# Output products two slots later, and the copy of the transposed maxima between two exponentials, in a kernel of two Fourier and two attention layers

## The chip, the cores and the metric

The kernel runs on one core of one Trainium2 chip. The metric is the device time of one execution in microseconds (us), the median of several. A profile of one execution stands beside it: a page of tables and a trace of every instruction. In its rows PE is the tensor engine (PEld are its weight loads), DVE the vector engine, ACT the scalar engine, POOL the GpSimd engine, and SP the queue from which the kernel issues nearly all of its transfers. [...]

## The reference

Four layers on a matrix of 2048 rows (tokens) and 640 columns: a Fourier layer (A), an attention layer (B), and both once more. Each adds its result to its input; in front of each stands a layer norm.

```python
def _A_ref(x, dft_seq_re, dft_seq_im, dft_hid_re, dft_hid_im):
    a = jnp.einsum("bsd,ed->bse", x, dft_hid_re)
    b = jnp.einsum("bsd,ed->bse", x, dft_hid_im)
    return jnp.einsum("ts,bse->bte", dft_seq_re, a) - jnp.einsum("ts,bse->bte", dft_seq_im, b)

def _B_ref(x, wqkv, wo):            # S = 2048, D = 640
    H = 32; Dh = D // H; W = 256    # 32 heads of 20 columns, a window of 256 rows
    q, k, v = ...                   # x @ wqkv, split by heads
    scores = jnp.einsum("bhqd,bhkd->bhqk", q, k) * (Dh ** -0.5)
    mask = (idx[:, None] - idx[None, :] >= 0) & (idx[:, None] - idx[None, :] < W)
    p = _softmax(jnp.where(mask, scores, -1e9))
    return jnp.einsum("bhqk,bhkd->bhqd", p, v)... @ wo

x = x + _A_ref(_layernorm(x), ...);  x = x + _B_ref(_layernorm(x), ...)
x = x + _A_ref(_layernorm(x), ...);  x = x + _B_ref(_layernorm(x), ...)
```

## The kernel before, in words

The Fourier layers are `spectral`, the attention layers `attention(0)` and `attention(1)`. Every product is made from fp16 halves (high and low part), three matmuls for one. All that the change touches lies in `attention`, which runs twice: from about 566 to 1070 us of the profiled span as layer 0, and from about 1580 us to the end as layer 1.

**Slots.** `attention` writes out its order by hand. Its main loop runs over `G`, and `now[0] = g = 2 * G` is the slot number; every pass takes two slots. The 2048 rows are cut into eight blocks of 256 rows (`b = g // 32`), and a pass works on four heads of 128 rows. A group of heads goes through a pipeline of passes:

- `scores(G)` and `largest(G)`: products of queries and keys, and their largest value for each row (DVE). After every second pass `part_tops` packs the maxima in fp16 halves (POOL, tile `tops`).
- `hand_on(n)`, HAND_LAG = 3 passes after the first of its two: PE turns the packed maxima (`hp`), ACT copies them to `ht` (L1176), SP stores `ht` to DRAM (`htd`). Two slots later `take_tops(n)` loads them as two extra rows of the query stack `qs` (`qs<-htd` in the trace), for which SP waits until the store has landed.
- `by_key(G)`, KEY_LAG = 8 passes behind: the scores once more, keys on the partitions, with the maxima subtracted by the two extra rows; then `probabilities(G, 1)` and `probabilities(G, 0)`, the two exponentials (ACT, L1211), behind which POOL masks the corners.
- `values(n)`, VALUE_LAG = 11: the products with v, the copy `pvs` (ACT), and `back(n)`, the turn back: PE turns the result to rows on partitions (`pf<-idf,pvs` in the trace), DVE divides by the sums (`r`, `o`), and POOL writes it in fp16 halves to `os` (a cast, L1262, and a subtraction, L1263). A block has eight groups `n`, so `back(8 * b + 7)` completes the block. `values(n)` stands in slot 4n + 22, and `back(n)` at the end of the same slot where a filler unit ran in it, else in the next pass.

**Filler units.** Beside this pipeline each pass runs one filler unit of 15 matmuls (`run_unit`; in some passes two, in some none). Kinds: `qk` (queries and keys of a block to come, 15 matmuls of 256 columns, `pf<-early,big`), `v` (`pf<-big,early`), `out` (the output product of 128 rows, two units, `pf<-bo,ot`, ended by DVE's `x` at L935), in layer 0 also `next` (first products of the next Fourier layer), and `last` (output products of the last block in three pieces of columns, 0-3, 3-4 and 4-5, made from PE transposes of `os`). A unit can be taken when its slot `at` has come and what it needs (`need`) is done; even passes prefer the wide kinds (all but `qk`), and of those the one with the smallest due slot goes first. In layer 1 the odd passes from slot 224 to 255 run no unit.

**Output of a block.** When `back` completes a block b below 7, it queues for each half m of the block (128 rows, number i = 2b + m)

```python
at, due, kind = now[0] + OUT_STEPS[0] + OUT_STEPS[2] * m, 2 * NP * (b + 2) + OUT_STEPS[1], ("out", b)
need = [(i - 2, 2)] if i > 1 else []
outs.append((at, need, partial(out_turn, i)))
fill.append(Unit(at, out_tile(i), kind, due + 3 * m + 2, [(i, 1)] + ["wo"] * (layer == 0)))
```

`out_turn(i)` is run by the loop in the first pass from slot `at` on in which the buffers allow it: SP issues a transposing DMA of `os` into `ot` (DMA_TRANSPOSE `ot<-os`) and the load `x<-x2d`. The unit `out_tile(i)` can be taken from six slots after `out_turn` (TURN_LAG). Within a pass SP gets first the store of `hand_on`, then the loads of `take_tops`, then the held loads of the stacks `qs` and `ks` (`qs<-qkd`, `ks<-qkd`), then `out_turn`. For the last block `back` queues the pieces as `last` units with a first slot of `now[0] + LAST_STEPS[0]`, at least 258 for the first half's early pieces and 272 for the second half.

**Orders.** PE's instructions and SP's loads are chained, so both keep the order in which the program writes them. On ACT, DVE and POOL a planner with costs of its own places instructions, unless a mark binds them: `in_line("act")` puts an instruction behind the last one that was marked on ACT. The exponentials are marked so, the copy L1176 is not.

Of the kernel before, what the change touches and what calls it, by code (L numbers as in the profile page):

```python
# [14 lines left out]
AF = mybir.ActivationFunctionType  # L15
# [21 lines left out]
FILL_LAST = 8  # L37
QK_SLOT = 20
NEXT_STEPS = (10, 22)
OUT_STEPS = (4, 40, 8)  # L40
LAST_STEPS = (1, 258)
LAST_FROM = 3
HAND_LAG = 3
KEY_LAG = 8
# [28 lines left out]
def body(ctx: ExitStack, tc: tile.TileContext, x_in, cmat, whid, wqkv, wo, out):  # L73
    nc = tc.nc
# [107 lines left out]
    def load(out, in_):  # L182
        with ExitStack() as order:
            if in_turn[0] and loads:
                order.enter_context(tc.issue_after(loads[-1]))
            elif floor:
                order.enter_context(tc.issue_after(floor[-1]))
            i = nc.sync.dma_start(out, in_)
        loads.append(i.ins)
# [17 lines left out]
    def new_f():  # L207
        return pf_.tile([P, 512], F32, tag="f", name="pf", bufs=2)
# [615 lines left out]
    def attention(layer, proj, dst, final):  # L824
        with ExitStack() as st:
# [294 lines left out]
            TOP, PT, topped, marks = {}, {}, [None], {}  # L1120

            @contextmanager
            def in_line(name):
                with ExitStack() as order:
                    if name in marks:
                        order.enter_context(tc.issue_after(marks[name]))
                    yield

            def place(g):

                b, r = divmod(g, 2 * NP)
                return 2 * b + r // 2 % 2, 2 * (r // 4) + r % 2
# [37 lines left out]
            def hand_on(n):  # L1170

                b, q = divmod(n, NP // 2)
                hp = new_f().bitcast(F16)[:16, :P]
                transpose(hp, tops[n % 2], idh)
                ht = sb.tile([16, P], F16, tag="ht", name="ht", bufs=3)
                nc.scalar.activation(ht, hp, AF.Copy)  # L1176
                load(ht_d[n % 4], ht)
                handed.append((now[0] + 2, partial(take_tops, n)))

# [21 lines left out]
            def probabilities(G, pi):  # L1201
                i, p0 = place(2 * G)
                first = max(0, 2 - i)
                n, k = divmod(G, 2)
                if k == 0 and pi:
                    PT[n] = sb.tile([P, 4, 6, P], F32, tag="ptq", name="ptq", bufs=2)
                q = PT[n]
                a0 = 3 * (i % 2)
                o = q[:, :, a0 + first:a0 + 3].rearrange("p (e l) a c -> p l e a c", e=2)
                with in_line("act"):  # L1210
                    marks["act"] = nc.scalar.activation(o[:, pi], tps[pi][:, :, first:], AF.Sigmoid, bias=shift, scale=alpha[:, 0:1]).ins  # L1211
                if pi:
                    return
                if i >= 2:
                    nc.gpsimd.affine_select(out=q[:, :, a0], in_=q[:, :, a0], pattern=[[0, 4], [-1, P]], base=0,  # L1215
                                            channel_multiplier=1, compare_op=OP.is_gt, fill=0.0)
                ins = nc.gpsimd.affine_select(out=q[:, :, a0 + 2], in_=q[:, :, a0 + 2], pattern=[[0, 4], [1, P]],  # L1217
                                              base=0, channel_multiplier=-1, compare_op=OP.is_ge, fill=0.0).ins
                if G == NG // 2 - 1 and not final:
                    hidden.after = ins  # L1220
# [24 lines left out]
            def back(n):  # L1245
# [20 lines left out]
                if last and d1 > k * 4 * DH // P and (d1 > 2 or k > LAST_FROM):  # L1266
                    for m in range(2):
                        step0 = max(now[0] + LAST_STEPS[0], NG + 2 * KEY_LAG if m else LAST_STEPS[1] if d1 < ND else 0)
                        fill.append(Unit(step0, last_out(2 * b + m, lastd[0], d1), "last", NS + 2 * d1 + m, [(2 * b + m - 2, 2)]))
                    lastd[0] = d1  # L1270
                elif k == NP // 2 - 1 and not last:
                    for m in range(2):
                        i = 2 * b + m
                        at, due, kind = now[0] + OUT_STEPS[0] + OUT_STEPS[2] * m, 2 * NP * (b + 2) + OUT_STEPS[1], ("out", b)
                        need = [(i - 2, 2)] if i > 1 else []
# [8 lines left out]
            def queue_qk(b):  # L1284
                for w in (1, 0):
                    for ct in range(ND):
                        need = [("rows", b, t) for t in range(2)] if b > 1 else []
                        fill.append(Unit(0, proj_qk(b, w, ct), ("qk", b), 2 * NP * (b - 1) + QK_SLOT, need, ns=15 * 109))
# [28 lines left out]
            for G in range(NS // 2 + 1):  # L1317
                now[0] = g = 2 * G
                b, r = divmod(g, 2 * NP)
                if g == NG:  # L1320
                    floor.append(loads[-1])
                if g < NG:
                    if r == 0:
                        flush(("qk", b))
                        if b == 0:
                            queue_qk(1)
                            queue_v(1)
                keyed = 0 <= G - KEY_LAG < NG // 2
                if g < NG:
                    scores(G, (0,))  # L1330
                if keyed:
                    by_key(G - KEY_LAG)
                if g < NG:
                    scores(G, (2, 1))
                if g < NG:
                    largest(G, 0)
                if keyed:
                    probabilities(G - KEY_LAG, 1)
                if g < NG:
                    largest(G, 1)  # L1340
                    if G % 2:
                        part_tops(G // 2)
                if keyed:
                    probabilities(G - KEY_LAG, 0)
                n = due(G, HAND_LAG)
                if n is not None:
                    hand_on(n)
                if turned_back:
                    with in_line("dve"):
                        back(turned_back.pop())  # L1350
                c = 2 if g == 0 else b + 3
                if g < NG and c < NBQ and (g == 0 or r == X2_STEP):
                    wanted.append(c)
                if wanted and x2s and g >= x2s[0] + 4 * (g > 0):
                    slow.append(rows_norm(wanted.pop(0), x2s.pop()))
                    x2s.clear()
                if slow:
                    normed_at[0] = g
                if wanted and not slow and not x2s and g >= normed_at[0] + FREE_STEPS:
                    x2s += [g, [keep.tile([P, D], F32, tag="res0", name="x2", bufs=2) for t in range(2)]]  # L1360
                    for t in range(2):
                        load(x2s[1][t], x2_d[2 * wanted[0] + t])
                if g < NG and r == ROWS_STEP:
                    flush(("v", b))
                    if b < NBQ - 2:
                        proj.new_rows(b + 2)
                        queue_qk(b + 2)
                        queue_v(b + 2)
                if g < NG and r == HIDDEN_STEP:
                    if b == NBQ - 1 and not final:  # L1370
                        flush(("v", b))
                        hidden = Hidden(xu_d)
                        pieces = hidden.pieces()
                        for k in range(2):
                            fill.append(Unit(g + NEXT_STEPS[k], hidden.stage(k, None), "next", NG + k))
                for _ in range(STEPS[layer][G % 2]):
                    slow_step()
                run_later()
                for _ in range(PIECES):
                    next(pieces, None)  # L1380
                while handed and handed[0][0] <= now[0]:
                    handed.popleft()[1]()
                run_held(1 << 20)
                if outs and outs[0][0] <= g and all(done.get(k, 1 << 20) + FREE_STEPS <= g for k in outs[0][1]):
                    outs.pop(0)[2]()
                n = due(G, VALUE_LAG)
                if n is not None:
                    for part in range(2):
                        values(n, part)
                    turned_back.append(n)  # L1390
                ran = False
                if not (G % 2 and NG - 2 * NP <= g < THIN_TO[layer]):
                    ran = run_unit(G % 2 == 0)
                if G % 2 and g < NG and left() and 2 * left() > must_to() - r:
                    ran = run_unit() or ran
                if ran and turned_back:
                    with in_line("dve"):
                        back(turned_back.pop())
# [40 lines left out]
```

## Time and profile before

| what | value |
|---|---|
| median of 3 runs (lowest to highest) | 2080.46 us (2077.89 to 2085.85) |
| the profiled execution: its time, its span | 2077.48 us, 2075.8 us |
| PE busy | 1991.0 us, 96% of the span |
| DVE, POOL, ACT busy | 1567.5, 1469.5, 1116.1 us |
| mean share of the 16 DMA engines, bytes moved | 50.5% in the main queue, 311.10 MB |
| mean granted clock of PE | 0.996 |

A row of the timeline has the start, the length, the engine, the line, the operation, out<-in by the program's names, the shapes, how many instructions were merged into the row, and in brackets the idle time of the engine before the row with what ended it. A row of SP tells how long the queue was with an issue, not how long the transfer took. In a row of a table by stretches stand, after the stretch and its length, the busy time of each engine with the number of instructions, then the granted clock of PE (1.00 is full speed), the share of the DMA engines and GB/s. All matmuls and transposes have line L126, a helper's, so they are told apart by their tiles.

### The profile page before, as it was taken

The page shows a single profiled execution, that of the slowest core. Times are in us where ns is not written, and L with a number is a line of the kernel's source. Part 1 is how long each engine was busy: PE and PEld are TensorE (multiplying, and loading weights), DVE is VectorE, ACT ScalarE, POOL GpSimd, SP SyncE. Part 2 cuts the span into 40 slices and gives each one's busy share as a digit, 9 for nine tenths or more (in the row PEclk, how much of TensorE's full clock was granted, in tenths as well). Part 3 has the DMA queues.
Part 4 walks back from the last instruction along what each step waited for, and adds up shares of the span by engine and source line. Part 5 has one row for each costly group of instructions (what it writes and reads, how often), then busy time and mean ns, then how long its engine had stood idle before and what let it go on. Part 6 is the DMA issues. An engine that isn't in the chain of part 4 may idle for free.

```text
span 2075.8 us, 55781 instructions
## 1 busy us (share of the span) xinstructions
PE 1991.0 (96%) x21881; PEld 1450.0 (70%) x21881; DVE 1567.5 (76%) x3261; ACT 1116.1 (54%) x1971; POOL 1469.5 (71%) x2162
## 2 busy tenths in 40 slices
PE   6999999999999999999989999999999989999997
PEld 4777777776766777777657777777677667777765
DVE  8888878768688898767538779777867878876682
ACT  5444555534257667766644444444342657666674
POOL 5777788868467777865547778777784767776653
PEclk9999999999999999999999999999999999999999
DMA  7556467565545354445435555454845455544232
GB/s 271 182 200 205 161 216 237 169 250 196 143 105 126 99 131 114 99 97 127 134 124 177 168 169 190 152 162 145 304 144 132 93 107 112 129 105 103 78 79 62
DMA packets 280508, 311.10 MB, mean 150 GB/s; under 512 B 107572, under 2 KB 214836, under 8 KB 271156
## 3 DMA queue, kind: packets, MB, share of 16 engines
q1 hardware_dynamic: 279668, 306.88, 50.5%
q8 instruction: 171, 2.80, 0.6%
q14 instruction: 93, 0.76, 0.1%
q10 hardware_dynamic: 576, 0.66, 0.1%
HBM read 201.72 MB, written 83.46 MB: 137 GB/s over the span
## 4 chain that ended last, share of the span: by engine, by line
PE 73%; DVE 13%; ACT 4%; issue 4%; DMA 3%; POOL 2%; SPq 0%; DVEq 0%; ACTq 0%; POOLq 0%
PE pf L126 32%; PE y L126 13%; PE x L126 12%; PE z L126 8%; PE sk L126 5%; PE sq L126 3%; DVE cc L536 3%; ACT ptq L1211 2%; DVE sq L1156 2%; DVE m L1158 2%; DMA res<-accd 1%; DVE res L559 1%; DVE lnt L151 1%; DVE lnst L139 1%; DVE x L935 1%
## 5 line engine op out<-in xcount | busy, mean ns | idle before, releaser
L126 PEld LDWEIGHTS <-cc 128*128 128x128 f16 x5376 | 524.4, 98 | 214.5 <-issue 14.8
L1211 ACT ACTIVATE ptq<-sk,shift,alpha 128x768 f32<-128x768 f32 (+2 forms) x512 | 471.9, 946 | 149.5 <-PE sk L126 76.0
L126 PEld LDWEIGHTS <-big 128*128 128x128 f16 x4320 | 412.4, 98 | 128.6 <-issue 24.3
L1158 DVE TENSOR_REDUCE m<-sq 128x2 f32<-128x512 f32 (+1 forms) x512 | 345.6, 675 | 19.1
L533 ACT ACTIVATE cc<-cs 128x512 f16<-128x512 f32 x256 | 153.7, 624 | 262.0 <-POOL cs L526 149.4
L126 PE MATMUL pf<-early,big 128*128 128x256 f16 x2400 | 289.2, 274 | 0.8 <-ACT qf L365 0.5
L1215 POOL TENSOR_SCALAR_AFFINE_SELECT ptq<-ptq 128x512 f32<-128x512 f32 x224 | 142.8, 637 | 186.8 <-ACT ptq L1211 185.6
L126 PE MATMUL y<-zc,cc 128*128 128x320 f16 x1728 | 262.8, 299 | 3.2 <-DVE pf L559 3.2
L536 DVE SCALAR_TENSOR_TENSOR cc<-cs,cc 128x512 f16<-128x512 f32 x256 | 249.5, 983 | 7.9 <-ACT cc L533 7.8
L1156 DVE COPY_PREDICATED sq<-mask,sk 128x256 f32<-128x256 int32 x448 | 189.4, 423 | 58.1 <-PE sq L126 56.8
L536 DVE SCALAR_TENSOR_TENSOR cc<-cq,cc 128x512 f16<-128x512 f32 x192 | 206.9, 1079 | 0.1
L126 PE MATMUL pf<-ptq,v 128*32 128x128 f32 (+1 forms) x3840 | 185.9, 332 | 8.1 <-DVE x L935 5.5
L126 PE MATMUL z<-zc,cc 128*128 128x320 f16 x1152 | 177.7, 299 | 6.6 <-DVE res L559 5.6
L126 PE MATMUL x<-zc,cc 128*128 128x320 f16 x1152 | 177.7, 299 | 0.0
L1217 POOL TENSOR_SCALAR_AFFINE_SELECT ptq<-ptq 128x512 f32<-128x512 f32 x256 | 166.3, 649 | 14.0 <-ACT ptq L1211 13.9
L126 PEld LDWEIGHTS pf<-ptq,v 128*32 128x32 f32 x3840 | 111.6, 111 | 53.2 <-DVE x L935 7.4
L365 ACT ACTIVATE qf<-pf 128x256 f32<-128x256 f32 x160 | 61.2, 383 | 157.2 <-PE pf L126 121.1
L126 PE MATMUL pf<-big,early 128*128 128x320 f16 x960 | 141.4, 300 | 1.0 <-ACT ht L1176 1.0
L525 POOL TENSOR_TENSOR cs<-cq 128x512 f32<-128x512 f32 x64 | 87.2, 1363 | 69.3 <-DVE cc L536 68.6
L126 PE MATMUL pf<-bo,ot 128*128 128x320 f16 x840 | 126.5, 304 | 8.4 <-DMA ot<-os 5.2
L126 PEld LDWEIGHTS <-qs 62*128 62x128 f16 x2688 | 90.8, 94 | 60.2 <-issue 55.7
L126 PEld LDWEIGHTS <-ot 128*128 128x128 f16 x960 | 90.4, 99 | 54.7 <-issue 6.8
(141 smaller groups left out, 3517.1 us busy)
## 6 DMA issues: line engine op xcount, KB each, us to landing
cq<-in_cmat_dram SPq DMA_DIRECT2D x64, 1024.0 KB
accd<-res SPq DMA_DIRECT2D x96, 320.0 KB
res<-accd SPq DMA_DIRECT2D x96, 320.0 KB
x<-x2d SPq DMA_DIRECT2D x64, 320.0 KB
qkd<-early SPq DMA_DIRECT2D x160, 128.0 KB
ks<-qkd SPq DMA_DIRECT2D x108, 160.0 KB
qs<-qkd SPq DMA_DIRECT2D x84, 160.0 KB
x2d<-res SPq DMA_DIRECT2D x32, 320.0 KB
```

Source lines behind the costliest of these rows:

```text
L126: i = getattr(nc.tensor, what)(*args, **kw)
L139: nc.vector.bn_stats(st[:, h], x[:, h * 320:(h + 1) * 320])
L151: ts(u, g, g, h, op0=OP.mult, op1=OP.mult)
L365: nc.scalar.activation(f, pf[:, :QB], AF.Copy, scale=down)
L525: g.tensor_tensor(s1, a21, a22, op=OP.add)
L533: nc.scalar.activation(cc[m][:, 0], f, AF.Copy, scale=C_UP)
L536: nc.vector.scalar_tensor_tensor(cc[m][:, 1], f, C_UP, cc[m][:, 0], op0=OP.mult, op1=OP.subtract)
L1156: marks["dve"] = nc.vector.copy_predicated(near[pi][:, :, 0], mask[:, None, :].to_broadcast([P, 2, P]), far).ins
L1158: marks["dve"] = nc.vector.tensor_reduce(TOP[n][:, pi, :, k], near[pi][:, :, :1 + (i >= 1)], axis=AX.XY, op=OP.max).ins
L1211: marks["act"] = nc.scalar.activation(o[:, pi], tps[pi][:, :, first:], AF.Sigmoid, bias=shift, scale=alpha[:, 0:1]).ins
L1215: nc.gpsimd.affine_select(out=q[:, :, a0], in_=q[:, :, a0], pattern=[[0, 4], [-1, P]], base=0, channel_multiplier=1, compare_op=OP.is_gt, ...
L1217: ins = nc.gpsimd.affine_select(out=q[:, :, a0 + 2], in_=q[:, :, a0 + 2], pattern=[[0, 4], [1, P]], base=0, channel_multiplier=-1, compare ...
```

## The change

Two constants and one place. The first slot of `out_turn` and of `out_tile` after a block's last turn back goes from 4 to 6 slots, and that of the pieces of the last block from 1 to 3. `hand_on` is called between the two exponentials instead of behind them, and its copy is bound in ACT's order: behind the first exponential by `in_line("act")`, and, since it sets the mark itself, ahead of the second.

```diff
-OUT_STEPS = (4, 40, 8)
-LAST_STEPS = (1, 258)
+OUT_STEPS = (6, 40, 8)
+LAST_STEPS = (3, 258)
...
@@ hand_on(n)
                 transpose(hp, tops[n % 2], idh)
                 ht = sb.tile([16, P], F16, tag="ht", name="ht", bufs=3)
-                nc.scalar.activation(ht, hp, AF.Copy)
+                with in_line("act"):
+                    marks["act"] = nc.scalar.activation(ht, hp, AF.Copy).ins
                 load(ht_d[n % 4], ht)
...
@@ the loop over G
-                if keyed:
-                    probabilities(G - KEY_LAG, 0)
                 n = due(G, HAND_LAG)
                 if n is not None:
                     hand_on(n)
+                if keyed:
+                    probabilities(G - KEY_LAG, 0)
```

## Prediction, made before the changed kernel ran

> **What bounds the kernel now.** First the page's busy times, then the table by stretches, then PE's own waits and, around them, the timeline.
>
> ```profile
> PE 1991.0 (96%) x21881; PEld 1450.0 (70%) x21881; DVE 1567.5 (76%) x3261; ACT 1116.1 (54%) x1971; POOL 1469.5 (71%) x2162
> ...
> 1000.00:1075.00 75.00, 63.29 (x726) 41.80 (x725) 28.67 (x68) 38.20 (x67) 34.76 (x63) 0.95 0.39 106
> ...
> 1600.00:1700.00 100.00, 89.36 (x1247) 64.67 (x1248) 81.83 (x195) 60.55 (x111) 67.02 (x141) 0.98 0.53 109
> ```
>
> PE works 96% of the span, and its work is not changed. Only its idle time can shrink, and the speed of its matmuls where the clock was halved. Most of the idle time that lies in attention stands in two stretches: 75.00 - 63.29 = 11.7 us where layer 0 ends, and 10.6 us early in layer 1, and the clock drops in both. PE's waits in the two attention layers have one long stop in each, on a transfer and on POOL (rows in parts 1 and 2). So the question is what the new slots do to these two, and what else they move.
>
> **Part 1: the first output unit of layer 1.** Block 0 is complete in slot 50; before, `out_turn(0)` stands in slot 54 and the unit out0 can be taken in slot 60, an even pass, which prefers it. The turn lands too late:
>
> ```profile
> 1671.63 0.37 SPq L188 DMA_DIRECT2D htd<-ht  x1
> ...
> 1672.82 0.38 PE L126 MATMUL pf<-idf,pvs 128*128 128x128 f32 x2
> ...
> 1672.93 3.23 SPq L196 DMA_TRANSPOSE ot<-os  x1
> ...
> 1676.20 0.58 SPq L188 DMA_DIRECT2D x<-x2d  x1
> ...
> 1677.51 1.09 SPq L188 DMA_DIRECT2D qs<-qkd  x2
> 1678.70 0.32 SPq L188 DMA_DIRECT2D htd<-ht  x1
> 1679.21 3.74 PE L126 MATMUL pf<-bo,ot 128*128 128x320 f16 x15 [5.23 <-DMA ot<-os]
> ...
> 1683.23 0.55 SPq L188 DMA_DIRECT2D qs<-htd  x2
> ...
> 1694.91 0.38 PE L126 MATMUL pf<-idf,pvs 128*128 128x128 f32 x2
> ...
> 1679.20:1682.90 3.70, 3.69 (x17) 2.01 (x19) 0.00 (x0) 0.00 (x0) 0.00 (x0) 0.57 0.52 106
> ```
>
> PE stands 5.23 us, and the unit then runs at 0.57 of the clock. After the change the turn stands in slot 56 and out0 is ready in slot 62. In slot 60 no wide unit is ready, so a qk unit of block 3 goes there; out0 takes slots 64 and 68, out1 slots 72 and 84 (before: 60 and 64, 68 and 84). The units of slots 60 to 72 are the same seven in another order. Layer 0 is a twin: out0 waits there for `wo`, and its slots 60 and 62 hold qk units, slot 64 a wide one:
>
> ```profile
> 654.40 0.38 PE L126 MATMUL pf<-idf,pvs 128*128 128x128 f32 x2
> ...
> 654.90 2.83 SPq L196 DMA_TRANSPOSE ot<-os  x1
> ...
> 658.12 0.31 PE L126 MATMUL sk<-ks,qs 62*128 62x128 f16 x4 [0.82 <-ACT ptq L1211]
> ...
> 659.06 1.03 SPq L188 DMA_DIRECT2D qs<-qkd  x2
> ...
> 660.65 1.81 PE L126 MATMUL pf<-early,big 128*128 128x256 f16 x15
> ...
> 664.39 0.27 PE L126 MATMUL sk<-ks,qs 62*128 62x128 f16 x3 [1.55 <-DVE o L1260]
> ...
> 665.15 2.21 PE L126 MATMUL pf<-big,early 128*128 128x320 f16 x15
> ...
> 671.17 0.38 PE L126 MATMUL pf<-idf,pvs 128*128 128x128 f32 x2
> ```
>
> From the turn back of group 9 to that of group 11 layer 0 takes 671.17 - 654.40 = 16.77 us, layer 1 takes 1694.91 - 1672.82 = 22.09 us. The difference is 5.32; of it 2.21 - 1.81 = 0.40 comes back in slot 72, which gets a wide unit for a qk one. That leaves 4.92.
>
> Two corrections. The 1.55 us in layer 0 are the first scores of block 2 (slot 64). The row names DVE, but the last rows of block 2's query stack were issued at 659.06, behind the turn (2.83) and its load, so I read it as that load. After the change these loads stand ahead of the turn, in both layers. I take 1.3 of the 1.55 as gained against the twin in each layer; the bounds are 0 (it is DVE) and 1.55. Against that, the turn now stands behind `qs<-htd` of slot 56, which waits for the store issued at 1671.63. The next store took 1683.23 - 1678.70 = 4.5 us to the load behind it, so SP is free at about 1676.1; 0.55 and 1.09 for two pairs of loads, and the turn is issued near 1677.8. It lands between 3.23 us (its issue alone) and 6.28 us (issue to PE's start, before) later: 1681.0 to 1684.1. PE comes to slot 64's unit at 1672.82 + (665.15 - 664.39) + (664.39 - 654.40) - 1.55 = 1682.0. So it may wait 0 to 2.1 us; I take 1.0. Layer 1: 4.92 + 1.3 - 1.0 = 5.2 us gained, bounds -0.3 (the full stop comes back in slot 64) to 7.3 (with the 1.55 and the 0.82 of the twin gone too). Layer 0: 1.3, bounds 0 to 1.55. The x load and both halves' turns move with `out_turn`; their first users are passes away, as out1 now starts in slot 72. Turns 2 and 3 of layer 1 and turn 12 of both layers move one pass as well, 13 in layer 1; no unit moves nearer to its turn than six slots, and I cost them at nothing, covered by those six slots.
>
> **Part 2: the end of layer 0.** `back(62)` stands in slot 270, and the piece last0:3-4 that needs its `os` could be taken at slot 271, so slot 272 begins with it:
>
> ```profile
> 1040.04 0.34 PE L126 MATMUL pf<-idh,os 128*128 128x128 f16 x3
> ...
> 1041.30 1.52 PE L126 MATMUL sq<-bo,ot 128*128 128x320 f16 x9
> ...
> 1045.99 1.51 PE L126 MATMUL pf<-ptq,v 128*32 128x256 f32 x32
> ...
> 1047.43 2.35 PE L126 MATMUL pf<-bo,ot 128*128 128x320 f16 x16
> ...
> 1049.24 1.26 POOL L525 TENSOR_TENSOR cs<-cq 128x512 f32<-128x512 f32 x1
> ...
> 1049.62 0.38 PE L126 MATMUL pf<-idf,pvs 128*128 128x128 f32 x2
> ...
> 1054.23 0.32 POOL L1262 CAST os<-o 128x160 f16<-128x160 f32 x1
> ...
> 1054.60 0.29 PE L126 MATMUL pf<-idh,os 128*128 128x128 f16 x1 [4.60 <-POOL os L1262]
> ...
> 1065.64 0.28 PE L126 MATMUL pf<-idh,os 128*128 128x128 f16 x2
> ...
> 1067.06 0.27 PE L126 MATMUL pf<-idh,os 128*128 128x128 f16 x2
> ...
> 1054.60:1061.50 6.90, 6.53 (x48) 3.33 (x49) 0.23 (x1) 0.28 (x1) 0.49 (x1) 0.53 0.01 2
> ```
>
> POOL has four sums of the next Fourier layer ahead of the cast, from 1049.24 to 1054.2, and PE stands 4.60 us, then works at 0.53 of the clock. After the change the piece is ready at 273, so slot 272 finishes out13 and goes on with last1:0-3, whose `os` columns are long there. Up to `back(63)` PE then has: 8 matmuls of out13 (half of 2.35, 1.2), six transposes with the wait for their copies (1041.30 - 1040.04 = 1.26), values 1.51, 16 matmuls 2.35: 6.3 us after 1050.0, that is 1056.3, past the cast. Then `back(63)` 0.38, two matmuls 0.3, the piece 1067.06 - 1065.64 = 1.42: last1:3-4 begins 8.4 us after 1050.0, where it now begins at 1065.64, 15.6 us after. Gain 7.2; I take 7.0 for a small wait on a PSUM bank. Bounds: 0 (the four sums then stand before a cast that is still needed at once) to 7.5. What follows, the next Fourier layer, hangs on PE's end here and moves with it.
>
> **Part 3: the end of layer 1.** Turn 13 moves from slot 256 to 258, so out13 runs in slots 264 and 266 instead of 262 and 266/268, and last0:0-3 in 268 and 270 instead of 264 and 266. Slot 262 is now without a unit beside slot 260, and slot 270 gets one. From 272 on nothing changes.
>
> ```profile
> 2040.48 0.61 PE L126 MATMUL sk<-qs,ks 62*128 62x128 f16 x12 [2.05 <-ACT ptq L1211]
> ...
> 2057.50 0.51 PE L126 MATMUL sk<-qs,ks 62*128 62x128 f16 x12 [0.86 <-ACT ptq L1211]
> ...
> 2060.25 0.44 PE L126 MATMUL pf<-idf,pvs 128*128 128x128 f32 x2 [0.80 <-ACT pvs L1243]
> ```
>
> The 0.86 and 0.80 of slot 270 get cover, 1.66 at most; the empty slot 262 costs between 0 (slot 262 has values) and a second 2.05. I take a gain of 0.8, the middle of 0 and 1.66.
>
> **Part 4: the copy.** In ACT's timeline 111 of the 128 copies stand between the two exponentials already, six come before any exponential (n = 0 to 2), and 11 stand behind both (n = 3 to 6 of each layer, 61 and 63 of layer 0, 63 of layer 1). One of the first kind, one of the last, and who waited for the copies in all:
>
> ```profile
> 696.79 0.25 ACT L1176 ACTIVATE ht<-pf 16x128 f16<-16x128 f16 x1
> 696.95 0.97 ACT L1211 ACTIVATE ptq<-sk,shift,alpha 128x768 f32<-128x768 f32 x1
> ...
> 2035.27 0.25 ACT L1176 ACTIVATE ht<-pf 16x128 f16<-16x128 f16 x1
> 2035.57 2.20 PE L126 MATMUL pf<-bo,ot 128*128 128x320 f16 x15 [0.40 <-ACT ht L1176]
> ...
>   PE pf L126: 2.0, 5
> ```
>
> Eleven copies come one exponential earlier and free PE's bank: at most 2.0 us gained. Eleven exponentials start 0.25 later: at most 2.8 lost. I take 0.5 gained.
>
> **Sum.** 5.2 + 1.3 + 7.0 + 0.8 + 0.5 = 14.8 us. The profiled execution took 2077.48 us, 2.98 below the median of 2080.46; that gives 2062.7 by the one and 2065.7 by the other. As the result is a median, I predict 2065. Bounds of the parts: all best, 7.3 + 1.55 + 7.5 + 1.7 + 2.0 = 20.0, gives 2057.5 from the profiled execution.
>
> **A rule about the clock.** In the rows above the clock stands at 0.57 and 0.53 behind stops of 5.23 and 4.60 us. The Trainium skill, page "TensorE: Matmul & The Clock Gate", section "Part 1: The HAM clock gate (the "warmup" mystery)", says that the clock halves after an idle window of about 3.4 us, and that the windows run freely, so that what a stop costs varies between runs. The trace agrees for these two stops. By that rule a median execution might not lose what this one lost to the half clock, 3.74 - 2.21 = 1.5 us in part 1 and up to 6.53 x (1 - 0.53) = 3.1 us in part 2; the sum would be 14.8 - 4.6 = 10.2. I keep 14.8, as the rows show both stops paid for.
>
> **The rivals.**
> - The turn lands late again and the stop moves to slot 64. For it: SP is late there, the store of slot 54 left at 1671.63, about when PE ended slot 58 (1672.82). Against it: PE wants the turn 8 slots after it instead of 6. Part 1 gives -0.3 in layer 1, the sum 9.3: 2071.
> - PE stops at the end of layer 0 all the same, because the planner puts the four sums before another cast. For it: POOL's order is the planner's. Against it: `back(62)` keeps its place, and there are 6.3 us of other work for PE. Sum 7.8: 2073.
> - The change does nothing that counts: both of these, 14.8 - 5.5 - 7.0 = 2.3: 2078.
> - Slower: SP's queue is blocked. The moved turns now stand behind the wait for a landed store and hold up the maxima of the next groups by 3.23 + 0.58 = 3.8 us each; if six of them (0 and 1 of layer 0, 0 to 3 of layer 1) make the products by key wait, 22.9 us are lost and only 8.3 of parts 2 to 4 are gained: 2095. It decides once the loads `qs<-htd` come more than their slack late: ten slots lie between `hand_on` and `by_key`, some 20 us (16.77 us for four passes above). Against it: SP is two passes late there today, and no long stop of PE is for these loads.
>
> **How the numbers follow.** Chances: forecast 0.58, the turn 0.13, the cast 0.13, nothing 0.08, slower 0.08. A measurement of this kernel tells some 0.5%, 10.4 us, from no change: the forecast lies beyond it, the first two rivals within, as does "nothing". With a little for a rival that lands beyond 10.4 us and a little for losses that I have not priced: faster 0.60, same 0.31, slower 0.09. The range goes from 2057, all parts at their best, to 2080, no change, which leaves out the slower case, half of "nothing" and a small tail below. The forecast alone: 2058 to 2070.
>
> **What would show it.** In PE's waits no `DMA ot<-os` of over 2.1 us, and out0 in the pass after the turn back of group 10; PE 94 us busy or more of 1600 to 1700; no 4.6 us stop on `os` near 1050, with last1:0-3 ahead of last0:3-4; a clock of 1.00 in both places; about 128 - 6 copies between exponentials. If the long stops are gone and the time is not down by 10 us, new stops of an order that I took as fixed, on POOL or ACT, make the prediction wrong.

## The result, and the profile after

| kernel | median (lowest to highest), us | the kernel before on the same chip | ratio, 95% interval |
|---|---|---|---|
| changed | 2057.98 (2057.23 to 2061.26) | 2078.24 | 0.9901, 0.9887 to 0.9914 |
| changed, measured again later | 2062.53 (2060.11 to 2066.07) | 2079.89 | 0.9921, 0.9906 to 0.9937 |

The change makes the kernel faster by 20.3 us in the first measurement and by 17.4 us in the second, each against the kernel before on the same chip; the forecast, 2065, was 15.5 below the median it started from (2080.46, of three executions). The profiled execution of the changed kernel took 2060.18 us, its span 2058.5: 17.3 below the span before.

The first row below is the page's busy times after; then come a table by stretches (the end of layer 0, and the 100 us that begin with the work that stood at 1600 before) and two rows of PE's waits in the attention layers and between them: in all, times, longest.

```profile
PE 1986.1 (96%) x21881; PEld 1448.5 (70%) x21881; DVE 1564.7 (76%) x3261; ACT 1114.6 (54%) x1971; POOL 1466.2 (71%) x2162
...
1000.00:1066.00 66.00, 59.45 (x722) 40.33 (x720) 28.08 (x68) 37.57 (x67) 34.35 (x63) 1.00 0.43 120
1591.00:1691.00 100.00, 94.38 (x1311) 68.93 (x1309) 84.75 (x201) 64.66 (x117) 71.94 (x152) 0.98 0.52 111
...
PE sk L126 <- ACT ptq L1212: 9.2, 19, 2.0
...
PE sq L126 <- ACT ot L1027: 2.5, 4, 1.6
```

PE's idle time is 2058.5 - 1986.1 = 72.4 us, before 2075.8 - 1991.0 = 84.8: 12.4 less. The same matmuls were busy for 4.9 us less. Together that is the 17.3. So nearly three quarters come from idle time and the rest from matmuls that no longer run at half clock. (PE's busy times are modelled.) At the end of layer 0 PE is idle for 66.00 - 59.45 = 6.6 us instead of 11.7, in the second stretch for 5.6 instead of 10.6. The two waits shown have the two longest single stops left in attention, 2.0 and 1.6 us; neither `os` nor `ot<-os` stops PE for long.

Where the time went is read from the turns back (`pf<-idf,pvs`). These are the first turn back of layer 1 and the last one of the kernel, before and then after:

```profile
1614.84 0.38 PE L126 MATMUL pf<-idf,pvs 128*128 128x128 f32 x2
2067.08 0.38 PE L126 MATMUL pf<-idf,pvs 128*128 128x128 f32 x2
```

```profile
1605.54 0.38 PE L126 MATMUL pf<-idf,pvs 128*128 128x128 f32 x2
2049.78 0.38 PE L126 MATMUL pf<-idf,pvs 128*128 128x128 f32 x2
```

The changed kernel is 9.3 us ahead where layer 1 begins and 17.3 at the end. The two timelines below show the places. First slots 54 to 68 of both layers, layer 0 and then layer 1:

```profile
655.24 0.38 PE L126 MATMUL pf<-idf,pvs 128*128 128x128 f32 x2
...
659.24 0.72 SPq L188 DMA_DIRECT2D qs<-qkd  x2
...
660.06 2.00 SPq L196 DMA_TRANSPOSE ot<-os  x1
...
663.45 0.48 PE L126 MATMUL sk<-ks,qs 62*128 62x128 f16 x4
...
670.58 0.38 PE L126 MATMUL pf<-idf,pvs 128*128 128x128 f32 x2
...
1664.92 0.38 PE L126 MATMUL pf<-idf,pvs 128*128 128x128 f32 x2
...
1668.59 0.98 SPq L188 DMA_DIRECT2D qs<-qkd  x2
...
1669.67 1.95 SPq L196 DMA_TRANSPOSE ot<-os  x1
...
1674.18 2.21 PE L126 MATMUL pf<-bo,ot 128*128 128x320 f16 x15
...
1681.15 0.38 PE L126 MATMUL pf<-idf,pvs 128*128 128x128 f32 x2
```

The last query-stack loads now leave ahead of the turn, the scores at 663.45 have no stop in brackets, and layer 0 takes 670.58 - 655.24 = 15.34 us where it took 16.77: 1.4 gained. In layer 1 out0 starts without a stop at 1674.18 and runs at full speed (2.21 instead of 3.74); 16.23 us where it took 22.09: 5.9 gained. In slots the turn stood six ahead of out0 and now stands eight. In time it left 1.1 us before PE came for it in the kernel before (1672.93, and 1679.21 - 5.23 = 1673.98), and now leaves 4.5 us before.

Then the end of layer 0:

```profile
1048.34 1.27 POOL L525 TENSOR_TENSOR cs<-cq 128x512 f32<-128x512 f32 x1
1048.72 0.38 PE L126 MATMUL pf<-idf,pvs 128*128 128x128 f32 x2
1048.94 1.25 PE L126 MATMUL pf<-bo,ot 128*128 128x320 f16 x8
...
1050.02 0.33 PE L126 MATMUL pf<-idh,os 128*128 128x128 f16 x3
...
1052.66 2.21 PE L126 MATMUL sk<-bo,ot 128*128 128x320 f16 x15
1053.36 0.32 POOL L1263 CAST os<-o 128x160 f16<-128x160 f32 x1
...
1056.87 0.28 PE L126 MATMUL pf<-idh,os 128*128 128x128 f16 x2
```

POOL still makes the four sums first and casts as late as before, 4.64 us after `back(62)` (before 1054.23 - 1049.62 = 4.61). But PE works through it on out13 and last1:0-3. last1:3-4 begins 1056.87 - 1048.72 = 8.2 us after `back(62)`, before 1065.64 - 1049.62 = 16.0: 7.9 gained.

The end of layer 1 gains another 3.5 us (part 3 below). The four places make 18.7, and 1.4 of it went elsewhere. The changed kernel's profile is 0.8 us behind at group 9 of layer 0. It loses 1.6 between the second and the third turn back of layer 1: 6.85 us there (1611.49 to 1618.34), before 5.23 (1620.79 to 1626.02). A window of half clock stands there that the profile of before hasn't:

```profile
1611.45:1614.87 3.42, 2.21 (x38) 1.00 1.00 259
1614.87:1618.28 3.41, 3.41 (x27) 0.50 0.07 22
```

Some 1.1 us came back in small steps.

### The profile page after: what moved, and what is told of

Same layout as the page of the kernel before. It is cut to its first block, busy times and chain, and to the rows that moved or that the text cites. A ratio compares the mean times of both kernels' runs of the same rounds, so it can differ in the third digit from the quotient of the medians.

```text
span 2058.5 us, 55778 instructions
## 1 busy us (share of the span) xinstructions
PE 1986.1 (96%) x21881; PEld 1448.5 (70%) x21881; DVE 1564.7 (76%) x3261; ACT 1114.6 (54%) x1971; POOL 1466.2 (71%) x2162
## 4 chain that ended last, share of the span: by engine, by line
PE 68%; DVE 15%; issue 5%; DMA 4%; ACT 4%; POOL 4%; SPq 1%; DVEq 0%; ACTq 0%; POOLq 0%
PE pf L126 32%; PE y L126 11%; PE x L126 10%; PE z L126 7%; PE sk L126 5%; DVE cc L536 4%; PE sq L126 3%; ACT ptq L1212 2%; DVE sq L1156 2%; DVE m L1158 2%; DMA res<-accd 2%; DVE res L559 1%; DVE lnt L151 1%; POOL cs L526 1%; DVE lnst L139 1%
## 5 line engine op out<-in xcount | busy, mean ns | idle before, releaser
L126 PE MATMUL x<-big 128*128 128x320 f16 x825 | 122.3, 299 | 2.0 <-DVE big L425 2.0
```

The lines of the kernel that those rows point to most:

```text
L126: i = getattr(nc.tensor, what)(*args, **kw)
```

## The experiments

The slots taken apart: each constant alone, the copy alone, and both constants without the copy.

```diff
-OUT_STEPS = (4, 40, 8)
+OUT_STEPS = (6, 40, 8)
```

> Only OUT_STEPS goes from 4 to 6; LAST_STEPS and the copy stay as before. Theory (three separate gains that add up): 1.4 us less in layer 0 before slot 64's scores, 5.9 less in layer 1 between the turns back of groups 9 and 11, and 0 to 3.4 less at the end of layer 1, where turn 13 moves one pass; in all 7 to 11 us, a median of 2067 to 2071 against 2078.2 before. The stop of 4.6 us on os at the end of layer 0 is still there. Rival (the constants work only together, because what is not used in one place is lost in the next): 2075 to 2078, with the stop on ot gone and another one in its place.

Measured: 2067.09 (2065.26 to 2068.09) against 2077.64, ratio 0.9946 (0.9934 to 0.9959), 10.5 us less. The one long stop left in attention is the other one:

```profile
PE pf L126 <- POOL os L1262: 4.6, 1, 4.6
```

```diff
-LAST_STEPS = (1, 258)
+LAST_STEPS = (3, 258)
```

> Only LAST_STEPS goes from 1 to 3; OUT_STEPS and the copy stay as before. Theory: the gain is at the end of layer 0 alone, 7.2 to 8.5 us, so a median of 2069 to 2071; the stop on ot in layer 1 (5.2 us) stays, and the end of layer 1 moves by -2 to +2. Rival (the cast behind the four sums only gives way because the other two edits shift POOL's order too): a stop on os of 3 us or more is still there and the median lies at 2075 to 2078.

Measured: 2070.35 (2066.91 to 2073.63) against 2077.64, ratio 0.9967 (0.9955 to 0.9979), 7.3 us less, with the mirror image in the waits:

```profile
PE pf L126 <- DMA ot<-os: 4.2, 1, 4.2
```

The two are separate and add up, as the theories of both runs had it: 0.9946 x 0.9967 = 0.9913, between the 0.9901 and the 0.9921 of the whole change. The rival of a gain that only both constants together make falls.

The copy alone (`hand_on` between the exponentials, bound by `in_line`), both constants as before:

> Only the copy's place between the exponentials; both constants as before. Theory: worth next to nothing, 0.5 us less with -2.0 and +2.8 as bounds: 2076 to 2081 by median, and both long stops stay. Rival (the copy carries what the two stops do not explain, some 3 to 5 us of the 20.3 between the kernels): 2073 to 2075, with shorter waits in many passes rather than in one place.

Measured: 2075.86 (2072.13 to 2081.47) against 2077.64, ratio 0.9990 (0.9980 to 0.9999). That is 1.8 us less, just below the theory's range and above the rival's; both long stops stay, as the theory said. And the constants without the copy:

> Both constants as in the changed kernel, the copy as before. Theory: the two constants are the change, 2058 to 2059 against 2058.0 of the changed kernel. Rival (the copy carries 3 to 5 us): 2061 to 2063.

Measured: 2062.20 (2060.61 to 2063.22), ratio 0.9923 (0.9911 to 0.9935). That is 4.2 us above the changed kernel's 2057.98, though not measured beside it, and spoke for the rival. So both ran once more, on one chip:

> The changed kernel once more, as the one to compare with on the same chip: 2057 to 2059 by both theories.

> Both constants without the copy's new place, once more, on the same chip as the changed kernel itself. Theory (the copy is worth what the traces show in single places: +0.46, -0.52 and -0.46 us at three turns back, and some of the wait in slot 64): 0.5 to 1.5 us above the changed kernel, and the 4.2 us between 2062.2 and 2058.0 are for the most part another chip and half clocks that fell otherwise. Rival (the copy is worth 3 to 5 us once both constants are set): 3 to 5 us above it here too.

Measured: 2062.53 with the copy, above the 2057 to 2059 that were expected, and 2062.04 (2060.59 to 2064.66) without it: neither what the theory nor what the rival said, but no 3 to 5 us. By its time the copy is worth nothing that this can tell, and the 4.2 us aren't the copy's. Why the changed kernel was faster the first time isn't settled; its second profile has five windows of half clock, the first two. The waits of PE show why the copy comes out nearly even. Without the copy (this run), then the changed kernel:

```profile
PE sk L126 <- ACT ptq L1211: 8.4, 17, 2.0
...
PE pf L126 <- ACT ht L1176: 1.9, 5, 0.5
```

```profile
PE sk L126 <- ACT ptq L1212: 9.2, 19, 2.0
...
PE pf L126 <- ACT ht L1177: 0.2, 1, 0.2
```

Five waits for the copy become one, 1.7 us less, and 0.8 of that comes back as longer waits for the exponentials (0.3 in the second profile of the changed kernel). The turns back say the same: every profile with the copy's new place loses 0.45 to 0.63 us between the first two of layer 0, and gains 0.52 or 0.53 between those of groups 56 and 57 there; from group 58 to 59 of layer 1 the copy alone and both profiles of the changed kernel gain 0.46 or 0.47. Without the new place these steps are 0.07 at most. Together that is some 0.5 gained.

What stops the scores in slot 64 of layer 0? The first try:

```diff
-hold(partial(load_stack, b, w, n), 2 * NP * (b - 1) + 2 * KEY_LAG + 4 * (1 - w) ..., 2 * n)
+hold(partial(load_stack, b, w, n), 2 * NP * (b - 1) + 2 * KEY_LAG + 2 * (1 - w) ..., 2 * n)
```

> The kernel before with one thing moved: the loads of the query stack start at slot 50 of the stretch instead of 52, so the last pair leaves in slot 54, ahead of the turn of ot, which stays in slot 54. Theory (the 1.55 us ahead of slot 64's scores in layer 0 are the last query-stack load, held up behind the turn on SP): that wait falls to 0.3 us or less with the turn where it was, 1.2 to 1.6 us less in layer 0; the stop on ot in layer 1 stays at 3.7 to 5.3 us; median 2075 to 2077.5 against 2077.6. Rival (it is DVE's product o, as the row names it): 1.2 to 1.8 us of wait are still there, and the time is that of before.

Measured: 2077.27 (2075.41 to 2084.95) against 2079.92, ratio 0.9992 (0.9979 to 1.0005). The edit moved nothing: the slot it lowers isn't what holds these loads back, the end of their last projection unit is, and SP's order came out the same. So this is the kernel before once more and decides nothing. The second try does move them:

```diff
-hold(partial(load_stack, b, w, n), ... + 4 * (1 - w) ..., 2 * n)
+hold(partial(load_stack, b, w, n), ... + 4 * (1 - w) ..., 2 * n * w)
```

> The kernel before with the three pairs of query-stack loads of a block all in one slot (the first pair's), so that all six stand ahead of the turn of ot in slot 54, which stays there. Theory (the 1.55 us ahead of slot 64's scores in layer 0 are the last of these loads, behind the turn): that wait is gone or under 0.3 us, though the turn has not moved; the stop on ot in layer 1 stays at 3 to 5.5 us; 1 to 2 us less, a median of 2076 to 2079 beside 2078 to 2080 of the kernel before. Rival (it is DVE's product o, as the row names it): 1.2 to 2.0 us of wait are still there.

Measured: 2083.09 (2080.17 to 2087.64) against 2079.89, ratio 1.0016 (1.0004 to 1.0028): slower. Its timeline, layer 0 and then layer 1:

```profile
657.23 2.79 SPq L188 DMA_DIRECT2D qs<-qkd  x6
...
661.20 2.72 SPq L196 DMA_TRANSPOSE ot<-os  x1
...
667.18 0.29 PE L126 MATMUL sk<-ks,qs 62*128 62x128 f16 x4
...
1679.93 2.86 SPq L196 DMA_TRANSPOSE ot<-os  x1
...
1686.45 3.92 PE L126 MATMUL pf<-bo,ot 128*128 128x320 f16 x14 [7.70 <-DMA ot<-os]
```

In layer 0 the stop ahead of the scores is gone while the turn stands in the same slot, and from the turn back of group 9 to that of group 11 it is 15.59 us where it was 16.77. So the stop was the load; the row that named DVE was a guess of the profile. In layer 1 six loads in a row hold the turn back further (it leaves 2.3 us after the turn back of group 9, before 0.1), and PE's stop on `ot` grows from 5.23 to 7.70 us. There the theory was wrong: it had expected the stop to stay at 3 to 5.5 and the kernel to be faster. The last row's unit has one more matmul, behind the end of the window that the view shows. The same few issues on SP decide both places: whichever stands behind is late.

Is it the slot of the turn, or the distance of six slots to its unit?

```diff
-OUT_STEPS = (6, 40, 8)
+OUT_STEPS = (8, 40, 8)
```

> The changed kernel with OUT_STEPS 8 instead of 6: the first turn stands in slot 58, and out0 of layer 1 still runs in slot 64, so six slots after its turn instead of eight. Theory (PE stopped on ot because six slots are too few for the turn where SP is late, whatever the slot): the stop on ot comes back in slot 64 of layer 1, 1.5 to 5 us, and with the tail of layer 0 in another order the median lies 1 to 6 us above the changed kernel, 2059 to 2064. Rival (slot 54 alone was bad, where store, query-stack loads and turn fall together; two slots later SP is clear): no stop on ot over 1 us, 2057 to 2059.

Measured: 2065.13 (2063.95 to 2065.87) against 2079.92, ratio 0.9932 (0.9909 to 0.9954). The time is above what either theory said. But the stop is not back, though out0 runs six slots behind its turn as before:

```profile
1672.64 2.66 SPq L196 DMA_TRANSPOSE ot<-os  x1
...
1677.36 2.21 PE L126 MATMUL pf<-bo,ot 128*128 128x320 f16 x15 [0.56 <-DMA ot<-os]
```

0.56 us instead of 5.23: slot 54 was the bad place, so the rival holds for this stop. Six slots are not a fixed time: the turn left 4.2 us before PE came for it here (1676.80), 1.1 us in the kernel before. The turn also lands sooner: PE starts 4.7 us after its issue, against 6.3 in the kernel before and 6.5 in the run with all loads at once. Why it lands sooner isn't settled. The time was lost for the most part at the end of layer 0, where out12, out13 and the pieces fall into other slots: by the turns back this kernel is 2.2 us ahead of the changed one at group 58 of layer 0 and 2.7 behind it where layer 1 begins. Two stops stand there that the changed kernel hasn't:

```profile
1041.75 1.40 PE L126 MATMUL sq<-bo,ot 128*128 128x320 f16 x9 [1.56 <-ACT ot L1027]
...
1052.14 0.23 PE L126 MATMUL pf<-idh,os 128*128 128x128 f16 x1 [1.15 <-POOL os L1263]
```

Is the cast's place behind the four sums all that stops PE at the end of layer 0? In the kernel before, for group 62 of layer 0 alone:

```diff
-nc.gpsimd.tensor_copy(hi, o)
-nc.gpsimd.tensor_tensor(lo, o, hi, op=OP.subtract)
+g = nc.vector if layer == 0 and n == NG // 4 - 2 else nc.gpsimd
+g.tensor_copy(hi, o)
+g.tensor_tensor(lo, o, hi, op=OP.subtract)
```

> The kernel before with the cast and the subtraction that write os for group 62 of layer 0 on DVE instead of POOL; all slots as before. Theory (only the four sums ahead of the cast on POOL make PE stop at the end of layer 0): PE's stop on os falls from 4.6 us to about 1.2 (o ends at 1050.7 in the profile of before, two DVE operations of 0.3 each, PE ready at 1050.0), the half clock behind it (6.8 us at half, 3.4 lost) goes, so 5 to 7 us less, a median of 2070.5 to 2072.5. Rival (PE waits there for something else as well, copies on ACT or a bank, and two slots of cover are what is needed): 0 to 3 us less, 2074.5 to 2077.5.

Measured: 2075.23 (2070.36 to 2081.76) against 2079.92, ratio 0.9979 (0.9964 to 0.9994), 4.7 us less than the kernel before: as a difference between theory and rival, as a median inside the rival's range. The timeline:

```profile
1049.48 1.26 POOL L527 TENSOR_TENSOR cs<-cq 128x512 f32<-128x512 f32 x1
1049.73 1.11 DVE L1263 CAST os<-o 128x160 f16<-128x160 f32 x1
1050.70 1.26 POOL L526 TENSOR_TENSOR cs<-cs,cq 128x512 f32<-128x512 f32 x1
1050.88 1.27 DVE L1264 TENSOR_TENSOR os<-o,os 128x160 f16<-128x160 f32 x1
...
1050.99 0.22 PE L126 MATMUL pf<-idh,os 128*128 128x128 f16 x1 [1.97 <-DVE os L1263]
...
1052.29 0.22 PE L126 MATMUL pf<-idh,os 128*128 128x128 f16 x1 [1.09 <-DVE os L1264]
```

The stop falls from 4.60 to 1.97 + 1.09 us, so POOL's queue was the cause, and what is left of the stop is for `os` too. It does not fall to 1.2, because the two operations, estimated at 0.3 each, took 1.11 and 1.27 on DVE. Each ends 0.1 to 0.2 us after one of POOL's sums ends (1050.74, 1051.96).

Two runs went for a faster kernel. The longest stop left in attention is the 2.05 us in slot 260 of layer 1, which runs no unit:

```diff
-THIN_TO = (240, 256)
+THIN_TO = (240, 260)
```

> The changed kernel with one more constant, THIN_TO of layer 1 from 256 to 260: slot 258 runs no unit, so the second half of out12 runs in the empty slot 260, ahead of the scores that wait 2.05 us for the exponentials there. Theory (the stop is a pass without a unit, and in the executions where it falls into one window of the clock it costs another 1.7 us of half clock): the 2.05 us stop goes or falls under 0.8, no half clock behind it, 1.5 to 3 us less than the changed kernel, a median of 2055 to 2056.5. Rival (slot 258, with values alone, gets the same stop): 2057.5 to 2059.

Measured: 2057.11 (2056.78 to 2058.72) against 2079.92, ratio 0.9895 (0.9873 to 0.9918). The median lies between theory and rival, and the changed kernel did not run beside it. The 2.05 us stop went as the theory said: the longest wait for an exponential is now 0.8. The piece last0:0-3 has the longest stop, and in this profile a window of half clock stands behind it:

```profile
PE sk L126 <- ACT ptq L1212: 7.5, 19, 0.8
...
PE sq L126 <- ACT ot L1027: 2.5, 4, 1.6
```

The last run adds to it that both copies of the transposes go to DVE in one piece:

```diff
-yield from turned(OS[i // 2][:, i % 2], k, ot, d0, d1)
+yield from turned(OS[i // 2][:, i % 2], k, ot, d0, d1, layer == 1 and i % 2 == 1 and d0 == 0)
...
-                if k:
+                if k or both:
```

> The kernel with the late second half of out12 (THIN_TO 260 in layer 1), and in the first piece of the last half block both copies of the transposes go to DVE, since ACT's stands behind two exponentials and PE waits 1.56 us for it. Theory: that stop falls under 0.6 us and no half clock follows it there; 1 to 3 us less than 2057.1, a median of 2054 to 2056. Rival (DVE's copy stands behind the products of the turn back, or the wait moves to the next exponentials): 2056.5 to 2058.

Measured: 2060.58 (2059.08 to 2063.66), on the chip where the changed kernel took 2062.53; ratios 0.9912 (0.9896 to 0.9929) and 0.9921. The edit hit the wrong half: the stop belongs to the first half's piece (`i` even), and it is still there, behind the same copy:

```profile
2038.96 0.49 ACT L1027 ACTIVATE ot<-pf 128x384 f16<-128x384 f16 x1
2039.51 1.40 PE L126 MATMUL sq<-bo,ot 128*128 128x320 f16 x9 [1.56 <-ACT ot L1027]
```

So this is the kernel with late out12 once more, but for one other copy that moved to DVE, some 2 us under the changed kernel where both ran together. The intervals overlap: the gain is likely, and not shown. The copy of the right half wasn't tried.

## Why the prediction was right, step by step

The prediction named the two long stops and what would end them; both went, and each by its own constant. The time came out 7 us below 2065, at the low edge of the range and just under the span of the forecast alone (2058 to 2070; the second measurement, 2062.53, lies inside). Of these 7 us, 2.2 lie in the median it started from, which is 2078.24 with six executions; between the profiled executions 14.8 were forecast and 17.3 measured.

- **Part 1, layer 1: 5.2 forecast, 5.9 measured.** Counted from the turn back of group 9, the turn was expected after 5.0 us and PE at the unit after 9.2; it left after 4.75 and PE came after 9.26. Mis-sized is the wait of 1.0 us: there was none, as the turn landed within 4.5 us of its issue, in the lower part of the 3.2 to 6.3 that were allowed. Against that the twin in layer 0 hid a wait: a `v` unit stands there, and behind out0 PE waits 0.74 us for DVE's `x` (L935). With these, the whole 1.55, and 0.14 from a shorter wait for an exponential (0.68, in the twin 0.82), the sum is 4.92 + 1.55 + 0.14 - 0.74 = 5.87.
- **Part 1, layer 0: 1.3 forecast, 1.4 measured.** That it was the query-stack load and not DVE is shown by the run with all these loads ahead of the turn.
- **Part 2: 7.0 forecast, 7.9 measured,** above the bound of 7.5. The mechanism is as told, to the place of the cast. The step that was short is the count up to `back(63)`: 8.4 us after 1050.0 is 8.8 after `back(62)`, where 8.2 passed. It added whole lengths of rows, and each row ends 0.06 to 0.17 us after the next has begun. The rival with the cast falls: its four sums still stand there, and PE doesn't meet them.
- **Part 3: 0.8 forecast, 1.2 to 2.0 measured.** The last turn back gained 17.3 us, and 13.8 of that were there after group 11 (1694.91 - 1681.15); 3.5 came between these two. Of the 3.5, 0.2 came in small steps up to group 58, 0.5 at group 59, where the wait of 0.40 for the copy is gone (part 4), and about 1.7 are one window of half clock that the profile of before has there and that of the changed kernel hasn't (below). 1.2 are left; the three other profiles with both constants and OUT_STEPS 6 that keep the empty slot 260, taken the same way, give 2.0. So the middle that was taken was too small. The 0.86 and 0.80 of slot 270 are gone, and the empty slot 262 cost a stop of 0.52 us, not a second 2.05.
- **Part 4: 0.5 forecast, some 0.5 by the turns back, nothing that the times can tell.** The waits agree with its bounds: 1.7 us off the one side, 0.3 to 0.8 back on the other.
- **The clock.** The forecast split 14.8 into 10.2 of idle time and 4.6 of half clock; the pages of the two profiles give 12.4 and 4.9. So both sources were there. The 4.6 were three windows of half clock behind the two long stops, and these are gone. That the sum agrees so well is in part luck: a fourth window, behind the stop in slot 260, went because the grid cuts that stop (below), and another came at 1614.87.
- **The rivals.** The turn late in slot 64, the cast, and SP's queue blocked: none of the three is in the trace. What SP does when it is blocked was seen in the run with all loads at once: a stop of 7.70 us.
- **The signs.** All were there (94.70 us busy in 1600 to 1700, 122 copies between exponentials) but one: the clock is 1.00 at the end of layer 0 and 0.98 in the second stretch, for the window at 1614.87.

## What to carry to other kernels

When one queue issues stores, loads and transposes in program order, and a load waits for a store to land, a distance counted in slots says little: look which issues stand between a wait and the transfer that PE needs, and how long before its user the transfer leaves (1.1 us here before, 4.5 after). Behind a late producer, try other work whose inputs are old before a faster producer: here that gave 7.3 us, the faster cast 4.7, with intervals that overlap. And test a reading of "what ended the wait" by moving that one thing: the name in the row, DVE's product here, can be wrong.

## What the runs showed of the hardware

**The windows of half clock lie on a fixed grid.** In each trace all half-clock stretches begin on one grid of 3.41 us. PE's busy time, the clock, the DMA share and GB/s, in consecutive windows of that grid around the same 2.05 us stop: the kernel before, then the changed kernel's first profile, then its second.

```profile
2037.35:2040.76 3.41, 1.36 (x29) 1.00 0.25 97
2040.76:2044.17 3.41, 3.41 (x43) 0.50 0.31 96
```

```profile
2021.05:2024.46 3.41, 2.96 (x37) 1.00 0.78 98
2024.46:2027.88 3.42, 1.82 (x44) 1.00 0.67 197
2027.88:2031.29 3.41, 2.89 (x36) 1.00 0.00 0
```

```profile
2026.86:2030.27 3.41, 1.36 (x33) 1.00 0.80 251
2030.27:2033.68 3.41, 3.41 (x44) 0.50 0.00 1
```

Where the whole stop lies in one window (1.36 busy, 2.05 idle), the next window runs at half clock and costs another 1.7 us. Where the grid cuts it (0.45 and 1.60 idle), nothing follows. The same kernel did both. Of the eleven profiles of this study that have this stop, nine have at least 1.96 us of it in one window, and a half clock behind it in each; in two the grid cuts it, and there is none. Idle time as the profile has it isn't the whole rule: the window above with 1.82 us busy has no half clock behind it, that at 1611.45 of the same profile, with 2.21 us busy, has. The Trainium skill, page "TensorE: Matmul & The Clock Gate", section "Part 1: The HAM clock gate (the "warmup" mystery)", has the free-running window of 3413 ns, and the traces agree with it; but it speaks of an idle window of about 3.4 us, and here 2.05 us were enough. This is one reason why the executions of one kernel spread: in the changed kernel's second profile the matmuls were busy for 3.9 us more than in the first (1990.0 against 1986.1), and its span is 5.8 us longer (2064.3 against 2058.5).

**Two operations on DVE were long beside POOL's sums.** A cast that takes 0.32 us on POOL took 1.11 on DVE beside POOL's sums, and ended 0.1 us after one; the subtraction took 1.27. The Trainium skill, page "SBUF — State Buffer", section "SBUF: two separate sides", says that the two engines share a port pair, and (under "Terms") that one of them holds it for its whole instruction; the rows of the run with the cast on DVE fit that. That the port is the cause isn't shown: no run has these two operations on DVE without POOL's sums beside them.
